# Two groups of tiled products per batch instead of three, with the scores and the slot reads moved into the h banks

## The chip, the cores and the metric

One core of one Trainium2 chip. The metric is device microseconds (us) of one execution; each kernel was run several times, and medians and ranges are given. Engines: PE is TensorE, DVE is VectorE, ACT is ScalarE, POOL is GpSimd, SP is SyncE (it issues most transposing transfers here). In the profile's lines PEld is the loading of weights into PE. The granted clock is the share of PE's full clock that the chip allowed. A run is called slow when it is more than 1.5% above the fastest of the same kernel. Medians and ranges are over all runs of a kernel unless it says otherwise; slow runs are left out of the ratios.

## The reference, cut to what matters

Eight batches of eight heads. Each batch has 512 tokens and 32 state slots per head. Tokens read the slots, slots read the tokens, and all rows then go through a two-layer expert with a squared ReLU.

```python
# x (8, 8, 512, 64), state (8, 8, 32, 64)
scores  = x @ state^T / sqrt(64);  a  = softmax(scores);   xread = a  @ state
scores2 = state @ x^T / sqrt(64);  a2 = softmax(scores2);  sread = a2 @ x
out = concat([xread, sread], axis=2)              # rows (8 * 544, 512)
h = out @ w_in                                    # (., 2048)
g = s * relu(h)**2 + b
return g @ w_out                                  # (., 512)
```

## The kernel before

Three things carry the argument.

First, `xread @ w_in` is never formed as such. With M = state @ w_in (per head, 32 rows each), h = a @ M. So each batch needs M in four pieces (`att_M`, PSUM tile `Mps`), the scores transposed (`att_T`, tile `T`), the slot reads (`att_V`, tile `V`), and then 16 blocks of h (`mm1_x`, two matmuls of 512 columns each). M, T and V are made with tiled products: several small matmuls side by side in the PE array. They are the only matmuls in a steady batch that use another tiling.

Second, the second layer uses a scheme of seven products of half-size sums (`fast_items`, tiles `oA`, `oB`, `oC`, sums `s`, weight sums `wd`). These 112 matmuls of 256 columns of the previous batch are spread over the current batch, seven after each h block.

Third, PSUM (the memory into which PE writes its results) is full. It has eight banks:

```python
psA = tile_pool(name="psA", bufs=2)   # "att": 2 buffers of two banks: T, Mps, V, D
psH = tile_pool(name="psH", bufs=2)   # "h":   2 buffers of one bank:  h blocks
psO = tile_pool(name="psO", bufs=2)   # "o":   2 buffers of one bank:  oA, oB, oC
```

What reads V is VectorE, which scales the slot reads by 1 / row sum (called "the scaling" below):

```python
def att_V(b):
    ps = att_ps([P, NG, D], FP32, f"V_{b}")          # a large buffer
    ...                                              # 32 matmuls of 64 columns
    for g in range(NG):
        nc.vector.tensor_scalar(a["sr"][:, g], ps[:, g], a["rq"][:, g : g + 1], None, ALU.mult)
```

VectorE also makes the token softmax of the next batch from the transposed exponentials ET (called "the shares"):

```python
def att_shares(b):
    with tc.issue_after(G["last"]):
        nc.vector.reduce_sum(den, ET_s, axis=X)               # 1.21 us
        nc.vector.reciprocal(inv, den)                        # 0.35 us
        nc.vector.tensor_mul(a["aT"], ET_s, inv.broadcast)    # 1.23 us
```

It is used from batch `NDT` = 4 on; earlier batches take their denominators from a matmul (`att_D`). The work of batch s (nb = s + 1 is the next batch) was placed so:

```python
at(3, att_T(nb));  at(3, att_M(nb, 0))        # group 1, after h(3)
at(7, att_M(nb, 1));  at(7, att_M(nb, 2))     # group 2, after h(7)
at(8, att_shares(nb));  at(9, att_a4_dma(nb))
at(10, att_V(s));  at(10, att_M(nb, 3))       # group 3, after h(10)
if s == 2: at(0, stT_dma)                     # transposed state of batches 3..7
...
for f in range(16):
    mm1_x(s, f)                               # h block f
    ... pieces of f ...
    ... seven second-layer matmuls of batch s - 1 ...
```

The softmax here doesn't subtract the row's maximum and nothing guards it: scores larger than these inputs give would overflow.

Of the kernel before, what the change touches and what calls it, by code (L numbers as in the profile page):

```python
# [14 lines left out]
def kernel(  # L15
# [10 lines left out]
    nc = tc.nc  # L26
# [19 lines left out]
    NDT = 4  # L46
# [162 lines left out]
    def att_T(b, gs):  # L209
        a = A[b]  # L210
        n = len(gs)
        T = att_ps([P, 2, 512], FP32, f"T_{b}_{gs[0]}")
        for q in range(NQ):
            for i, g in enumerate(gs):
                h = head_of(g, q)
                for m in range(2):
                    mm(
                        T[32 * q : 32 * q + 32, m, 256 * i : 256 * i + 256],
                        st_of(b, h, m),
                        a["xT"][64 * m : 64 * m + 64, h].rearrange("p k t -> p (k t)"),  # L220
                        tp=(64 * m, 32 * q),
                    )
        if gs[0] == 0:
            a["E"] = apool.tile([P, NG, S], FP16, name=f"E_{b}", tag="E", bufs=3)
            a["rs"] = apool.tile([P, NG], FP32, name=f"rs_{b}", tag="rs", bufs=4)
        for i, g in enumerate(gs):
            nc.scalar.activation(  # L227
                a["E"][:, g, :].rearrange("p (m t) -> p m t", m=2),
                T[:, :, 256 * i : 256 * i + 256],
                AF.Exp,  # L230
                scale=scale,
                accum_out=a["rs"][:, g : g + 1],
            )
# [44 lines left out]

    def att_M(b, c, how):
# [17 lines left out]
        if how == "split":  # L297
            nc.vector.tensor_copy(dst[:, 0], two[0])  # L298
            (nc.vector.tensor_copy if c in (0, 3) else nc.scalar.copy)(dst[:, 1], two[1])
        elif how == "act":  # L300
            nc.scalar.copy(dst, ps)  # L301
        else:
            nc.vector.tensor_copy(dst, ps)

    def att_ET(b):
        a = A[b]
        a["ET"] = apool.tile([P, NG * SCH, P], FP16, name=f"ET_{b}", tag="ET", bufs=3)
        nc.sync.dma_start_transpose(out=a["ET"], in_=a["E"].rearrange("p g t -> p (g t)"))
        a["rq"] = apool.tile([P, NG], FP32, name=f"rq_{b}", tag="rq", bufs=4)
        nc.vector.reciprocal(a["rq"], a["rs"])  # L310

    def att_V(b):
        a = A[b]
        ps = att_ps([P, NG, D], FP32, f"V_{b}")
# [43 lines left out]
    def mm1_close(key, hps, ntok, f):  # L358
# [3 lines left out]
        if key == 0 and f in (1, 5):  # L362
            nc.vector.tensor_scalar(r16[:, f % 2], hps, 0.0, None, ALU.max)
        else:
            nc.scalar.activation(r16[:, f % 2], hps, AF.Relu)  # L365
        if f % 4 == 0:
# [293 lines left out]
    with tc.manual_schedule(engines={ET.PE, ET.SP, ET.Pool}):  # L660
# [90 lines left out]
        def pieces(s):  # L751
# [5 lines left out]

            if s == 1:
# [3 lines left out]
                at(0, lambda: att_ET(1))  # L762
                at(8, lambda: att_xT_dma(3))
# [18 lines left out]
            if s == 2:  # L782
                at(0, stT_dma)
            if nb < B:
                at(3, lambda: att_T(nb, [0, 1]))
                at(3, lambda: att_M(nb, 0, "act"))
                at(4, lambda: att_ET(nb))
                if s in (2, 3):
                    at(4, lambda: att_xT_dma(nb + 1))
                if s >= 3 and s + 3 < B:  # L790
                    at(13, lambda: att_xT_dma(s + 3))
                if nb < NDT:
                    at(5, lambda: att_D(nb, [0, 1]))
                else:
                    at(8, lambda: att_shares(nb))
                    at(9, lambda: att_a4_dma(nb))
                at(7, lambda: att_M(nb, 1, "act"))
                at(7, lambda: att_M(nb, 2, "act"))
# [4 lines left out]
            at(10, lambda: att_V(s))  # L803
# [4 lines left out]
            if nb < B:  # L808
                at(10, lambda: att_M(nb, 3, "act"))
# [8 lines left out]
        for s in range(1, B):  # L818
# [13 lines left out]
            for f in range(NKF):  # L832
                mm1_x(s, f)
# [80 lines left out]
```

## Time and profile before

| | before |
|---|---|
| median of 3 runs | 210.69 us (210.08 to 210.84) |
| profiled span, granted clock | 208.0 us, 1.00 |
| PE / DVE / ACT / POOL busy | 96% / 78% / 60% / 18% |
| batch 2 (first h to first h) | 23.24 us |
| batches 3, 4, 5, 6 | 21.27 us each |
| from the first h of batch 7 to the last matmul | 43.50 us |

The lines themselves are in the prediction. A batch is measured from its first h matmul to that of the next. A "gap" in this document is the start of a matmul, less the start of the run of matmuls before it and its streaming time (0.216 us for 512 columns, 0.109 us for 256). The profile's own "idle" column is some 0.16 us smaller, because it models the end of a matmul later.

One more view of the kernel before is needed for the comparison. It is the timeline of VectorE in batch 4 around the scaling (columns: start, duration, engine, line, operation, output and input). The V matmuls of this batch began at 110.60 us.

```profile
110.02 1.23 DVE L265 TENSOR_TENSOR aT<-ET,inv 128x1024 f16<-128x1024 f16 x1
111.17 0.68 DVE L371 TENSOR_TENSOR g<-r 128x1024 f16<-128x1024 f16 x1
111.77 0.74 DVE L528 SCALAR_TENSOR_TENSOR osb<-oC,s_bc,u 128x512 f32<-128x512 f32 x1
112.43 0.47 DVE L328 TENSOR_SCALAR sr<-V,rq 128x64 f16<-128x64 f32 x2
```

Here 2.30 us pass from V's first matmul to the end of the scaling. V lies in one of the two large buffers and the next batch's T takes it only after the boundary.

### The profile page before, as it was taken

What the parts mean: (1) busy time and instruction counts of PE and PEld (TensorE: products, weight loads), DVE (VectorE), ACT (ScalarE), POOL (GpSimd) and SP (SyncE); (2) the same over time, 40 slices, a digit from 0 to 9 for tenths busy, and PEclk for the clock granted to TensorE, in tenths of its full rate; (3) what the DMA queues carried; (4) which work ended last, traced back from release to release, by engine and by line L of the source; (5) the groups of instructions that cost most, each with busy time, mean ns of one, the idle gap of its engine ahead of it and who ended that gap; (6) DMA issues with size and microseconds to landing.
All of it is one profiled execution on the core that took longest, in us unless ns stands there. A gap on an engine that the chain in (4) does not pass through costs nothing.

```text
span 208.0 us, 4757 instructions
## 1 busy us (share of the span) xinstructions
PE 199.5 (96%) x1947; PEld 129.4 (62%) x1947; DVE 162.1 (78%) x282; ACT 125.3 (60%) x218; POOL 37.6 (18%) x64
## 2 busy tenths in 40 slices
PE   7888999999899999999999999999999999999992
PEld 2433343445566676667666766676667777788882
DVE  1587825978769796899779977998799877895862
ACT  3678865698489557765776477656774544533100
POOL 5970001501110330123011201120111012100210
PEclk9999999999999999999999999999999999999999
DMA  5999996999947299979833915231324111110143
GB/s 183 225 202 206 207 191 104 179 181 174 266 52 153 72 194 123 124 163 185 127 103 67 196 52 102 54 107 54 101 29 132 50 54 50 54 50 0 54 145 111
DMA packets 45946, 25.35 MB, mean 122 GB/s; under 512 B 30884, under 2 KB 43940, under 8 KB 45924
## 3 DMA queue, kind: packets, MB, share of 16 engines
q0 software_dynamic: 15536, 16.19, 38.8%
q1 hardware_dynamic: 29588, 8.49, 23.8%
q10 hardware_dynamic: 800, 0.36, 0.7%
q8 instruction: 15, 0.25, 0.5%
q14 instruction: 7, 0.06, 0.1%
HBM read 17.33 MB, written 8.91 MB: 126 GB/s over the span
## 4 chain that ended last, share of the span: by engine, by line
PE 82%; DVE 6%; DMA 6%; ACT 4%; issue 1%; POOL 0%; SPq 0%; POOLq 0%
PE h L70 23%; PE oB L70 17%; PE oC L70 12%; PE oA L70 10%; PE o L70 6%; PE Mps L70 4%; DMA wi<-in_moe_w_in_dram 4%; PE h_sr L70 3%; DMA stT_all<-st 2%; ACT r L365 2%; DVE g L371 1%; PE T L70 1%; PE oB_sr L70 1%; PE V L70 1%; DVE M L298 1%; PE oA_sr L70 1%
## 5 line engine op out<-in xcount | busy, mean ns | idle before, releaser
L365 ACT ACTIVATE r<-h 128x512 f16<-128x512 f32 x126 | 74.4, 601 | 52.0 <-PE h L70 51.4
L70 PE MATMUL h<-a,M 128*128 128x512 f16 x256 | 75.0, 379 | 0.9 <-DVE M L298 0.6
L371 DVE TENSOR_TENSOR g<-r 128x1024 f16<-128x1024 f16 x64 | 44.1, 691 | 16.0 <-ACT r L365 15.8
L70 PEld LDWEIGHTS <-s 128*128 128x128 f16 x448 | 42.8, 98 | 19.3 <-issue 3.7
L70 PEld LDWEIGHTS <-g 128*128 128x128 f16 x400 | 38.0, 98 | 18.9 <-issue 2.9
L536 POOL DMA_DIRECT2D out_dram<-osb x27 | 18.2, 675 | 125.5 <-DVE osb L528 120.3
L70 PE MATMUL oB<-wd,s 128*128 128x256 f16 x224 | 32.7, 273 | 0.0
L70 PE MATMUL oA<-wo,g 128*128 128x256 f16 x224 | 31.6, 273 | 0.1
L70 PEld LDWEIGHTS <-M 128*128 128x128 f16 x256 | 24.6, 98 | 10.9 <-DVE M L298 1.6
L301 ACT CAST M<-Mps 128x1024 f16<-128x1024 f32 x27 | 26.8, 1017 | 1.4 <-PE Mps L70 0.8
L70 PE MATMUL oC<-wd,s 128*128 128x256 f16 x112 | 16.5, 273 | 0.0
L70 PE MATMUL o<-wo,g 128*128 128x512 f16 x64 | 16.3, 380 | 0.0
L70 PE MATMUL oB<-wd,g 128*128 128x256 f16 x112 | 15.9, 273 | 0.0
L70 PE MATMUL oC<-wo,s 128*128 128x256 f16 x112 | 15.3, 273 | 0.0
L365 ACT ACTIVATE r_sr<-h_sr 128x256 f16<-128x256 f32 x16 | 6.1, 382 | 8.4 <-PE h_sr L70 8.4
L227 ACT ACTIVATE E<-T 128x512 f16<-128x512 f32 x16 | 9.4, 596 | 1.2 <-PE T L70 1.1
L471 DVE TENSOR_TENSOR s<-s,g 128x1024 f16<-128x1024 f16 x14 | 9.7, 691 | 0.4
L70 PE MATMUL h_sr<-srdT,wi 128*128 128x256 f16 x64 | 9.6, 273 | 0.0
L465 DVE TENSOR_TENSOR s<-g 128x1024 f16<-128x1024 f16 x14 | 9.6, 685 | 0.0
L473 DVE TENSOR_TENSOR s<-g,s 128x1024 f16<-128x1024 f16 x14 | 9.6, 684 | 0.0
L469 DVE TENSOR_TENSOR s<-g,g 128x1024 f16<-128x1024 f16 x14 | 9.6, 683 | 0.0
L528 DVE SCALAR_TENSOR_TENSOR osb<-oC,s_bc,u 128x512 f32<-128x512 f32 x12 | 8.9, 746 | 0.5 <-PE oC L70 0.5
(102 smaller groups left out, 187.4 us busy)
## 6 DMA issues: line engine op xcount, KB each, us to landing
out_dram<-osb POOLq DMA_DIRECT2D x31, 256.0 KB, 2.8
xn<-in_x_dram POOLq DMA_DIRECT2D x7, 512.0 KB, 7.0
wi<-in_moe_w_in_dram POOLq DMA_DIRECT2D x4, 512.0 KB, 9.2
wo<-in_moe_w_out_dram POOLq DMA_DIRECT2D x4, 512.0 KB, 15.9
xf<-in_x_dram SPq DMA_DIRECT2D x2, 512.0 KB, 4.8
out_dram<-osb_sr SPq DMA_DIRECT2D x8, 32.0 KB, 1.6
out_dram<-osb_sr ACTq DMA_DIRECT2D x8, 32.0 KB, 1.7
out_dram<-osb_last SPq DMA_DIRECT2D x2, 128.0 KB, 1.9
```

The source lines that it names most:

```text
L70: return nc.tensor.matmul(out, lhsT, rhs, start=start, stop=stop, tile_position=tp, is_transpose=is_transpose, skip_group_check=True,)
L227: nc.scalar.activation(a["E"][:, g, :].rearrange("p (m t) -> p m t", m=2), T[:, :, 256 * i : 256 * i + 256], AF.Exp, scale=scale, accum_ou ...
L298: nc.vector.tensor_copy(dst[:, 0], two[0])
L301: nc.scalar.copy(dst, ps)
L365: nc.scalar.activation(r16[:, f % 2], hps, AF.Relu)
L371: nc.vector.tensor_mul(gt[:, f % 4 - 1 : f % 4 + 1], r16, r16)
L465: nc.vector.tensor_sub(o, a11, a21)
L469: nc.vector.tensor_add(o, a21, a22)
L471: nc.vector.tensor_sub(o, SQ[b, 1, j], a11)
L473: nc.vector.tensor_sub(o, a12, SQ[b, 2, j])
L528: nc.vector.scalar_tensor_tensor(osb, acc[bank], s_bc, add, ALU.mult, ALU.add)
L536: nc.gpsimd.dma_start(dst[j][:, :, n0 : n0 + NH], osb)
```

## The change

Its intent: switching the array between tilings costs time, so do it twice a batch and not three times. For that the scores take the two h banks (one per half, exponentials split in four), V takes one h bank, and the two large buffers are left for two pieces of M. Batch 3 uses the transposed softmax too (`NDT` = 3), and the state transposes are issued a batch earlier. The core of the diff:

```diff
-    NDT = 4
+    NDT = 3
@@ att_T
+        one_bank = b >= NDT
+        if one_bank:
+            Ts = [psH.tile([P, NG, S // 2], FP32, tag="h", name=f"T_{b}_{m}") for m in range(2)]
...
+        if one_bank:                       # four exponentials of 256 columns
+            for m in range(2):
+                for g in gs:
+                    nc.scalar.activation(a["E"][:, g, 256 * m : 256 * m + 256], Ts[m][:, g, :], AF.Exp, ...)
@@ att_V
-        ps = att_ps([P, NG, D], FP32, f"V_{b}")
+        if b >= NDT - 1:
+            ps = psH.tile([P, NG, D], FP32, tag="h", name=f"V_{b}")
+        else:
+            ps = att_ps([P, NG, D], FP32, f"V_{b}")
@@ pieces(1)
+                at(7, stT_dma)
                 at(8, lambda: att_xT_dma(3))
@@ pieces(s), s >= 2
-            if s == 2:
-                at(0, stT_dma)
-                at(3, lambda: att_T(nb, [0, 1]))
-                at(3, lambda: att_M(nb, 0, "act"))
+                ahead(4, lambda: att_M(nb, 0, "later"))
+                ahead(4, lambda: att_T(nb, [0, 1]))
+                ahead(4, lambda: att_M(nb, 1, "later"))
...
-                at(7, lambda: att_M(nb, 1, "act"))
-                at(7, lambda: att_M(nb, 2, "act"))
-            at(10, lambda: att_V(s))
+            ahead(10, lambda: att_V(s))
+                ahead(10, lambda: att_M(nb, 2, "later"))
+                ahead(10, lambda: att_M(nb, 3, "later"))
-                at(10, lambda: att_M(nb, 3, "act"))
@@ the loop over f
+                for fn in todo_s.get((f, "ahead"), []):
+                    fn()
+                if s > 1 and f >= 4:       # the seven second-layer matmuls now come before h(f)
+                    for fn in items[f]:
+                        fn()
+                    items[f] = []
                 mm1_x(s, f)
```

"later" means that the matmuls of M come in the group and the copy out of PSUM a few h blocks after it. The shares stay at f = 8 and 9.

More of the change, by code (lines that the diff above doesn't have):

```diff
@@ L210, in att_T @@
         a = A[b]
-        n = len(gs)
-        T = att_ps([P, 2, 512], FP32, f"T_{b}_{gs[0]}")
+        one_bank = b >= NDT
+        if one_bank:
+            Ts = [psH.tile([P, NG, S // 2], FP32, tag="h", name=f"T_{b}_{m}") for m in range(2)]
+        else:
+            T = att_ps([P, 2, 512], FP32, f"T_{b}_{gs[0]}")
+            Ts = [T[:, m, 0 : 256 * len(gs)].rearrange("p (g t) -> p g t", t=256) for m in range(2)]
         for q in range(NQ):
@@ L217, in att_T @@
                     mm(
-                        T[32 * q : 32 * q + 32, m, 256 * i : 256 * i + 256],
+                        Ts[m][32 * q : 32 * q + 32, i, :],
                         st_of(b, h, m),
@@ L224, in att_T @@
             a["E"] = apool.tile([P, NG, S], FP16, name=f"E_{b}", tag="E", bufs=3)
-            a["rs"] = apool.tile([P, NG], FP32, name=f"rs_{b}", tag="rs", bufs=4)
+            n = 2 * NG if one_bank else NG
+            a["rs"] = apool.tile([P, n], FP32, name=f"rs_{b}", tag="rs", bufs=4)
+        if one_bank:
+            for m in range(2):
+                for g in gs:
+                    nc.scalar.activation(
+                        a["E"][:, g, 256 * m : 256 * m + 256],
+                        Ts[m][:, g, :],
+                        AF.Exp,
+                        scale=scale,
+                        accum_out=a["rs"][:, NG * m + g : NG * m + g + 1],
+                    )
+            return
         for i, g in enumerate(gs):
@@ L277, in att_a4_dma, with copy_M @@
         )
+    def copy_M(dst, ps):
+        with tc.issue_after(G["relu"]):
+            nc.scalar.copy(dst, ps)
     def att_M(b, c, how):
@@ L296, in att_M @@
         dst = a["M"][:, :, FC * c : FC * c + FC]
-        if how == "split":
+        if how == "later":
+            a["M", c] = lambda: copy_M(dst, ps)
+        elif how == "split":
             nc.vector.tensor_copy(dst[:, 0], two[0])
@@ L309, in att_ET @@
         a["rq"] = apool.tile([P, NG], FP32, name=f"rq_{b}", tag="rq", bufs=4)
-        nc.vector.reciprocal(a["rq"], a["rs"])
+        rs = a["rs"]
+        if b >= NDT:
+            rs = apool.tile([P, NG], FP32, name=f"rt_{b}", tag="rt")
+            nc.vector.tensor_add(rs, a["rs"][:, 0:NG], a["rs"][:, NG : 2 * NG])
+        nc.vector.reciprocal(a["rq"], rs)
     def att_V(b):
         a = A[b]
-        ps = att_ps([P, NG, D], FP32, f"V_{b}")
+        if b >= NDT - 1:
+            ps = psH.tile([P, NG, D], FP32, tag="h", name=f"V_{b}")
+        else:
+            ps = att_ps([P, NG, D], FP32, f"V_{b}")
         for g in range(NG):
@@ L365, in mm1_close @@
             nc.scalar.activation(r16[:, f % 2], hps, AF.Relu)
+            G["relu"] = nc.cur_bb.bb.instructions[-1]
         if f % 4 == 0:
@@ L756, in at, with ahead @@
                 out.setdefault(f, []).append(fn)
+            def ahead(f, fn):
+                out.setdefault((f, "ahead"), []).append(fn)
             if s == 1:
@@ L781, in pieces @@
                 at(13 if s == 2 else 2, lambda: load_x(s + 3))
-            if s == 2:
-                at(0, stT_dma)
             if nb < B:
-                at(3, lambda: att_T(nb, [0, 1]))
-                at(3, lambda: att_M(nb, 0, "act"))
+                ahead(4, lambda: att_M(nb, 0, "later"))
+                ahead(4, lambda: att_T(nb, [0, 1]))
+                ahead(4, lambda: att_M(nb, 1, "later"))
                 at(4, lambda: att_ET(nb))
-                if s in (2, 3):
+                at(4, lambda: A[nb]["M", 0]())
+                at(6, lambda: A[nb]["M", 1]())
+                if s == 3:
                     at(4, lambda: att_xT_dma(nb + 1))
-                if s >= 3 and s + 3 < B:
-                    at(13, lambda: att_xT_dma(s + 3))
-                if nb < NDT:
-                    at(5, lambda: att_D(nb, [0, 1]))
-                else:
-                    at(8, lambda: att_shares(nb))
-                    at(9, lambda: att_a4_dma(nb))
-                at(7, lambda: att_M(nb, 1, "act"))
-                at(7, lambda: att_M(nb, 2, "act"))
+                at(8, lambda: att_shares(nb))
+                at(9, lambda: att_a4_dma(nb))
+                if s == 2:
+                    at(9, lambda: att_xT_dma(nb + 1))
+                elif s + 3 < B:
+                    at(13, lambda: att_xT_dma(s + 3))
             if s == 2:
@@ L802, in pieces @@
                 at(12, lambda: att_srT_dma(1))
-            at(10, lambda: att_V(s))
+            ahead(10, lambda: att_V(s))
+            if nb < B:
+                ahead(10, lambda: att_M(nb, 2, "later"))
+                ahead(10, lambda: att_M(nb, 3, "later"))
+                at(10, lambda: A[nb]["M", 2]())
+                at(12, lambda: A[nb]["M", 3]())
             if s == last_b:
@@ L807, in pieces @@
                 at(12, lambda: att_srT_dma(s))
-            if nb < B:
-                at(10, lambda: att_M(nb, 3, "act"))
             if s == last_b:
```

## The prediction

> **What bounds the kernel now.** I read the page first, then the busy time by stretch, then the matmuls in order of time over one batch, then VectorE (DVE) at a batch boundary.
>
> The page and, with it, the list of waits:
>
> ```profile
> PE 199.5 (96%) x1947; PEld 129.4 (62%) x1947; DVE 162.1 (78%) x282; ACT 125.3 (60%) x218; POOL 37.6 (18%) x64
> ...
> PE 82%; DVE 6%; DMA 6%; ACT 4%; issue 1%; POOL 0%; SPq 0%; POOLq 0%
> ...
> PE T L70 <- DMA stT_all<-st: 0.8, 1, 0.8
> ```
>
> TensorE (PE) carries 82% of the chain that ended last, and the only wait that the change names is a single one of 0.8 us for the transposed state. A busy PE is not yet a full PE, so I took batches. A batch starts at its first h matmul: 52.26, 75.50, 96.77, 118.04, 139.32 and 160.59 us for batches 2 to 7. The stretches between them:
>
> ```profile
> 52.26:75.50 23.24, 22.42 (x261) 14.89 (x259) 18.66 (x33) 16.06 (x26) 3.50 (x5) 1.00 0.64 136
> 75.50:96.77 21.27, 21.27 (x227) 14.58 (x224) 18.68 (x31) 14.17 (x25) 3.61 (x5) 1.00 1.03 154
> 96.77:118.04 21.27, 21.27 (x226) 14.59 (x224) 18.67 (x31) 14.16 (x25) 3.60 (x5) 1.00 0.65 127
> ```
>
> (Columns after the length: busy PE, weight loads, DVE, ACT, POOL.) Three things to see: 21.27 us repeats to the hundredth, PE is never idle in it, and DVE is 18.7 of 21.3 us busy, 88%, so it has little room. That PE streams at its rate and doesn't merely look busy comes from the sum: 32 h matmuls at 0.216 us (the pairs below are 0.43 apart) are 6.9 us, 112 matmuls of 256 columns at 0.109 us (seven are 0.76) are 12.2 us, and 2.1 us is left for the tiled products T (scores), Mps and V. All of the steady stages can give lies in those 2.1 us. They are, in batch 4:
>
> ```profile
> 104.63 0.59 PE L70 MATMUL h<-a,M 128*128 128x512 f16 x2
> 105.06 0.82 PE L70 MATMUL oB<-wd,s 128*128 128x256 f16 x6
> ...
> 105.82 0.59 PE L70 MATMUL h<-a,M 128*128 128x512 f16 x2
> 106.35 0.63 PE L70 MATMUL Mps<-wi,stT_all 64*32 64x512 f16 x16
> 106.91 0.94 PE L70 MATMUL oC<-wd,s 128*128 128x256 f16 x7
> ...
> 110.60 0.42 PE L70 MATMUL V<-xn,ET 128*32 128x64 f16 x32
> 110.95 0.41 PE L70 MATMUL Mps<-wi,stT_all 64*32 64x512 f16 x8
> 111.29 0.94 PE L70 MATMUL oB<-wd,g 128*128 128x256 f16 x7
> ```
>
> Two h matmuls take 0.43 us, so the array was through at 106.25 and the tiled group began at 106.35: 0.10 us to enter. The 16 Mps need 2 x 0.213 us of streaming (eight tiles side by side, 512 columns each, at the h rate) and last 0.56: 0.13 us to leave. One group thus costs about 0.23 us beyond its work, three times a batch (T with one Mps; two Mps; V with one Mps).
>
> **What the Trainium skill says.** "TensorEngine Tiling (Array Packing)", section Tiling Modes (Key Properties): "Changing tiling mode (not just tile) drains the TensorE". The trace agrees, at the 0.10 and 0.13 us above. The same page, section Restrictions and Gotchas (PSUM Pressure), says that different row tiles may not use one PSUM bank at once; that is why the scores still take two banks when they move to h. "TensorE: Matmul & The Clock Gate", section Back-to-back issue gap, gives N/2.4 + 2.5 ns, or 216 ns for 512 columns: the trace has 0.43 us for two. No run shows the drain apart from its group.
>
> **The change part by part.**
> 1. Three groups become two: M0, T, M1 before h(4), and V, M2, M3 before h(10). Saved: one enter and leave, 0.23 us a batch. Batches 2 to 6 prepare a next batch: 5 x 0.23 = 1.15 us, all on PE, all on the path.
> 2. Batch 3 no longer forms its softmax denominators by matmul: two D matmuls in batch 2 go, 0.43 us of PE. ACT loses one log and one exponential of 1.0 us each (off the path), DVE loses a product (0.68) and gains what the later batches have, a sum, a reciprocal and a product of 1.21 + 0.35 + 1.23 us. DVE in batch 2 goes from 18.7 to about 20.8 us of some 22: 95%.
> 3. The state transposes: in the queue of SyncE they now stand ahead of the x transposes that were issued at 46.21 us, which waited for their load, in a queue idle from 39.5 us. The transposes take 4.6 us to land; they can be there by about 48 and are needed at 57. The gap before T of batch 3 was 57.45 - 56.06 - 0.43 = 0.96, of which 0.10 is the entry: 0.86 us saved.
>
> Sum of the gains: 1.15 + 0.43 + 0.86 = 2.44 us, which makes 208.2. Moving M's copies and splitting the exponentials (four of 256 columns for two of 512, an estimated 0.3 us more on ACT) is off the path, ACT being 67% busy. The score banks: the group begins about 0.8 us (seven matmuls) after h(3), M0 goes first, and h(3)'s activation is done by then. After T come M1 and seven products, 1.1 us in all, before h(4) wants a bank; two exponentials at an estimated 0.36 us and 0.3 us of delay need 1.0. It just fits.
>
> **What it gives back.** From h(4) on, the seven products of the previous batch now come before each h pair and no longer after. So h(15) comes 0.76 us later, measured from those products. At the boundary stands this chain on DVE:
>
> ```profile
> 96.84 0.69 DVE L371 TENSOR_TENSOR g<-r 128x1024 f16<-128x1024 f16 x1
> 97.44 0.75 DVE L554 SCALAR_TENSOR_TENSOR qa<-oA,s_bc,bias_bc 128x512 f32<-128x512 f32 x1
> 98.11 0.68 DVE L469 TENSOR_TENSOR s<-g,g 128x1024 f16<-128x1024 f16 x1
> 98.82 0.69 DVE L471 TENSOR_TENSOR s<-s,g 128x1024 f16<-128x1024 f16 x1
> ...
> 99.57 0.67 PEld L70 LDWEIGHTS <-s 128*128 128x128 f16 x7 [0.31 <-DVE s L471]
> ```
>
> h(15) began at 95.57, its products were wanted at 99.59, and the weights came at 99.57: no slack at all. In the new order PE is there 4 x 0.43 + 2 x 0.76 = 3.25 us after h(15). If qa moves ahead of g (its matmuls now end before h(15)), the chain is 1.27 (h to g) + 0.71 + 0.71 + 0.75 = 3.44. So I expect a new wait of 0.2 us at each of five boundaries, 1.0 us, and up to 0.3 in the tail, where such a chain exists too.
>
> **Rivals.**
> (a) No new wait at all: 208.2. For it: the items were placed with care, and PE-bound stages repeat exactly. Against it: the boundary chain has no slack.
> (b) DVE becomes what releases PE. V's result now lies in an h bank until DVE has scaled it. In batch 4, V began at 110.60 and its second scaling ended at 112.90, behind the 2.86 us of the shares. In the new order V comes about 1.2 us earlier against h(9) and the shares don't, so its bank may come free some 1.4 us after h(11) wants it. How bad depends on which of the two banks h(11) gets. A clue is that oB at 103.11 began while oA's bank was still to be read (osb, 103.31), so banks go to whichever is free, not in turn; then h(11) takes h(10)'s bank at 0.1 us of delay, perhaps 0.2 more for h(12). Five times 0.1 to 0.3 is 0.5 to 1.5 us; five times 1.4, 7 us, would be the bad end, 217.
> (c) In batch 2 there is a third tiled group, V of batch 1, whose bank M3 needs 2.0 us later. If the scaling stands behind batch 3's new shares, PE waits about 1.7 us there, once; I give this a little over half.
> (d) The state transposes, going out earlier, delay the load of x for batch 3 and with it its transposes. Landing at most 8.5 us after 46.21, these have over 2 us to spare: unlikely.
>
> **Range and chances.** 2.44 us of gain is sure work removed; 1.0 at the boundaries I count in full; about 0.2 for the tail, and I weigh (b) and (c) at half or less of their middle values because the placing looks tuned: 0.5 + 0.5 together, less 0.5 since a late PE at one wait shortens the next. Net 2.44 - 1.0 - 0.2 - 0.5 = 0.74, rounded up a little for that tuning: 209.8 us, 0.9 off 210.69. The best case is 208.2; two bad waits give 212 to 213. Range 207.9 to 212.3. Faster by 2% would be below 206.5, beyond the sum of all gains: 2%. Slower by 2% is above 214.9, which takes the bad end of (b): 4%.
>
> **What would show it.** Right: batches 3 to 6 take 21.27 - 0.23 + the waits; two tiled groups a batch, each with 0.10 and 0.13 around it; T of batch 3 without its wait; a wait for the second-half sums (L471) of about 0.2 us at the third product run of each batch. If that wait isn't there and batches take 21.04, (a) holds. If h(11) or h(12) waits for DVE's scaling of V and batches take 22 or more, (b). If the last Mps of batch 2 waits for a scaling, (c). The prediction is wrong if the group overhead doesn't fall with the number of groups, or if DVE's order at the boundary puts qa behind g, which makes each wait 0.85 us.

## The result, and the profile after

The changed kernel took 217.25 us (median of 4 runs, 216.91 to 218.45, all fast). The kernel before took 210.76 us in the same rounds. The ratio is 1.0324 (95% interval 1.0278 to 1.037): slower. Ratios here are the mean time of one kernel's fast runs over that of the other's fast runs of the same rounds, so they are not quite the ratio of the medians quoted. The predicted range ended at 212.3.

The page of the changed kernel, its busy times and the chain that ended last:

```profile
PE 200.9 (93%) x1945; PEld 129.6 (60%) x1945; DVE 163.4 (76%) x289; ACT 123.9 (57%) x236; POOL 37.6 (17%) x64
...
PE 53%; DVE 28%; ACT 8%; issue 6%; DMA 3%; DVEq 0%
```

PE's share of the chain fell from 82% to 53%, and VectorE's rose from 6% to 28%. VectorE is no busier as a share of the span than before (76% against 78%). It has become what PE waits for, without being full.

The busy times by batch of the changed kernel, batches 2 to 5 (columns as in the prediction; batch 6 took 22.61 us):

```profile
52.48:75.60 23.12, 22.05 (x259) 14.87 (x257) 19.67 (x36) 13.71 (x27) 3.42 (x6) 1.00 0.62 120
75.60:98.47 22.87, 21.44 (x225) 14.57 (x224) 18.90 (x33) 14.29 (x28) 4.77 (x7) 1.00 0.94 164
98.47:122.31 23.84, 21.61 (x225) 14.57 (x224) 18.73 (x32) 14.29 (x28) 3.17 (x5) 1.00 0.66 112
122.31:144.92 22.61, 21.44 (x225) 14.58 (x224) 18.64 (x32) 14.29 (x28) 2.70 (x4) 1.00 0.39 90
```

Batches that took 21.27 us, with PE busy all the time, now take 22.6 to 23.8, with PE idle for more than a microsecond. VectorE's work in them is the same 18.6 to 18.9 us. The list of waits of the changed kernel names the cause (columns: total, times, longest):

```profile
PEld L70 <- DVE sr L357: 7.1, 5, 2.0
PE h L70 <- DVE sr L357: 4.7, 4, 1.7
PE oB L70 <- DVE s L501: 1.2, 5, 0.5
DVE den L278 <- DMA ET<-E: 1.1, 1, 1.1
PE Mps L70 <- DVE sr L357: 1.0, 1, 1.0
```

An h matmul waits four times for `sr`, the scaling that empties V's bank. The third product run (oB) waits five times for the half sums. M's last piece waits once for the scaling of batch 1. In the timeline of PE in batch 5 of the changed kernel one sees which h block it is:

```profile
135.16 0.59 PE L70 MATMUL h<-a,M 128*128 128x512 f16 x2
135.68 0.42 PE L70 MATMUL V<-xn,ET 128*32 128x64 f16 x32
136.03 0.63 PE L70 MATMUL Mps<-wi,stT_all 64*32 64x512 f16 x16
136.59 0.94 PE L70 MATMUL oB<-wd,g 128*128 128x256 f16 x7
137.36 0.59 PE L70 MATMUL h<-a,M 128*128 128x512 f16 x2
...
138.12 0.60 PE L70 MATMUL oC<-wo,s 128*128 128x256 f16 x4
139.70 0.60 PE L70 MATMUL h<-a,M 128*128 128x512 f16 x2 [0.98 <-DVE sr L357]
```

The group itself is as planned: V, then two pieces of M, in one stretch. h(10) at 137.36 gets the free h bank. h(11) could have begun at 138.12 + 4 x 0.109 = 138.56; it began at 139.70, a gap of 1.14 us. VectorE's timeline in the same stretch says why:

```profile
135.45 1.21 DVE L278 TENSOR_REDUCE den<-ET 128x32 f32<-128x1024 f16 x1
136.58 0.74 DVE L558 SCALAR_TENSOR_TENSOR osb<-oC,s_bc,u 128x512 f32<-128x512 f32 x1
137.24 0.34 DVE L280 RECIPROCAL inv<-den 128x32 f16<-128x32 f32 x1
137.50 0.63 DVE L401 TENSOR_TENSOR g<-r 128x1024 f16<-128x1024 f16 x1
138.04 1.21 DVE L281 TENSOR_TENSOR aT<-ET,inv 128x1024 f16<-128x1024 f16 x1
139.17 0.47 DVE L357 TENSOR_SCALAR sr<-V,rq 128x64 f16<-128x64 f32 x2
```

VectorE works without a pause and in a fixed order. V is complete at about 136.0, but the scaling stands behind the three steps of the shares, an eviction and a square, and ends at 139.64. The scaling takes 0.47 us; V's bank is held for 3.96 us from its first matmul. Before it was 2.30 us, and in a bank that nobody needed.

At the boundary to batch 6 the chain of squares and half sums looks so on VectorE in the changed kernel:

```profile
145.25 0.74 DVE L584 SCALAR_TENSOR_TENSOR qa<-oA,s_bc,bias_bc 128x512 f32<-128x512 f32 x1
145.91 0.68 DVE L401 TENSOR_TENSOR g<-r 128x1024 f16<-128x1024 f16 x1
146.62 0.69 DVE L499 TENSOR_TENSOR s<-g,g 128x1024 f16<-128x1024 f16 x1
147.35 0.69 DVE L501 TENSOR_TENSOR s<-s,g 128x1024 f16<-128x1024 f16 x1
```

and so on PE:

```profile
147.31 0.59 PE L70 MATMUL h<-a,M 128*128 128x512 f16 x2
148.10 0.94 PE L70 MATMUL oB<-wd,s 128*128 128x256 f16 x7 [0.19 <-DVE s L501]
```

As predicted, qa has moved ahead of g. The last half sum ends at 148.04. PE was through with h(2) at 147.31 + 0.43 = 147.74 and began its products at 148.10, a gap of 0.35 us.

The batches add up from these gaps. With -0.23 us for the group that went:

| batch | before | group and other gains | boundary | h(4) | wait of h(11), with oC before it | sum | measured |
|---|---|---|---|---|---|---|---|
| 3 | 21.27 | -0.23 | +0.61 | +0.08 | +1.14 | 22.87 | 22.88 |
| 4 | 21.27 | -0.23 | +0.35 | +0.08 | +1.89 + 0.48 | 23.84 | 23.84 |
| 5 | 21.27 | -0.23 | +0.35 | +0.08 | +1.14 | 22.61 | 22.61 |
| 6 | 21.27 | -0.23 | +0.35 | +0.08 | +1.14 | 22.61 | 22.61 |

In batch 4 the transposed exponentials landed late (the wait of `den` above), the shares and all behind them with it. In batch 2 the gains are larger (-0.84 for the state transposes' wait, -0.43 for the two D matmuls, -0.23 for a group) and +1.23 for M's last piece, 0.08 at h(11) and 0.06 at h(4) take nearly all of them back: 23.12 against 23.24. The tail is 0.55 us longer (44.05). The rest of the 7.6 us of span is 0.2 us ahead of batch 2 and 0.1 after the last matmul.

### The profile page after: what moved, and what is told of

It is laid out like the page before. It is cut to its first block, busy times and chain, and to the rows that moved or that the text cites. A ratio compares the mean times of both kernels' runs of the same rounds, so it can differ in the third digit from the quotient of the medians.

```text
span 215.6 us, 4780 instructions
## 1 busy us (share of the span) xinstructions
PE 200.9 (93%) x1945; PEld 129.6 (60%) x1945; DVE 163.4 (76%) x289; ACT 123.9 (57%) x236; POOL 37.6 (17%) x64
## 4 chain that ended last, share of the span: by engine, by line
PE 53%; DVE 28%; ACT 8%; issue 6%; DMA 3%; DVEq 0%
PE h L70 12%; PE oB L70 10%; PE o L70 7%; DVE g L401 7%; PE oA L70 6%; ACT r L394 5%; PE oC L70 3%; DVE s L499 3%; DMA ET<-E 3%; PE h_sr L70 3%; DVE s L501 3%; PE warm_ps L70 3%; PE Mps L70 3%; DVE osb L558 2%; DVE aT L281 2%
## 5 line engine op out<-in xcount | busy, mean ns | idle before, releaser
L401 DVE TENSOR_TENSOR g<-r 128x1024 f16<-128x1024 f16 x64 | 43.6, 683 | 21.8 <-ACT r L394 21.6
L297 ACT CAST M<-Mps 128x1024 f16<-128x1024 f32 x20 | 20.1, 1007 | 0.0
L234 ACT ACTIVATE E<-T 128x256 f16<-128x256 f32 x20 | 7.4, 383 | 4.0 <-PE T L70 4.0
```

Of the source, the lines that this page charges most:

```text
L234: nc.scalar.activation(a["E"][:, g, 256 * m : 256 * m + 256], Ts[m][:, g, :], AF.Exp, scale=scale, accum_out=a["rs"][:, NG * m + g : NG * ...
L297: nc.scalar.copy(dst, ps)
L401: nc.vector.tensor_mul(gt[:, f % 4 - 1 : f % 4 + 1], r16, r16)
```

## The experiments

My theory after the result: VectorE's queue releases V's h bank too late, and h(11) happens to be given that bank. The rivals: the early state transposes disturb the transfers; the new order of products at the batch boundary costs the time; the tiled groups cost more than thought.

Each label is followed by its edit, what was expected, and what came. All timed runs are set against the kernel before on the same chip (medians between 209.97 and 210.51).

### Is it V's bank, and is it VectorE's queue?

**e12_bank.** The changed kernel with the two h banks named. They are handed out in turn, except that h(11) is given the bank that h(10) had. The instruction order on every engine was compared and is the same as in the changed kernel. The edit is shortened: T, V and the other users of the h banks go through `h_bank` as well.

```diff
-        return pool.tile([P, ntok], FP32, tag=tag, name=f"h_{key}_{f}")
+        same = key != "sr" and key >= 2 and f == 11
+        return h_bank([P, ntok], name, same)     # tags h0 and h1, one buffer each, in turn
```

> The changed kernel with the two h banks named, and the eleventh h chunk given the bank of the tenth and not that of V; the instructions of every engine and their order are the same. Theory (the bank that h(11) got is the step that failed): its wait of 1.14 us (1.89 in batch 4) falls to about 0.1, h(12) waits 0 to 0.2 for V's bank, and 0.8 to 1.0 us a batch comes back in batches 3 to 6, less if the boundary waits grow: 213 to 214. Rival (VectorE is late whatever the bank): the boundary waits grow by as much, 216.5 or more.

Measured: 215.01 us (213.93 to 216.29), ratio 1.0212 (1.0162 to 1.0263). PE in batch 5 of this kernel:

```profile
138.50 0.60 PE L70 MATMUL oC<-wo,s 128*128 128x256 f16 x4
139.02 0.59 PE L70 MATMUL h<-a,M 128*128 128x512 f16 x2
139.45 0.93 PE L70 MATMUL oC<-wo,s 128*128 128x256 f16 x7
```

The same h(11), after the same four products, has a gap of 0.08 us in place of 1.14 (138.94 to 139.02). h(12) waited 0.28 and 0.69 us in batches 3 and 4 and not at all in 5 and 6. So the bank handed to h(11) made the wait. But the batches came to 21.84 to 22.71 us, not to 21.5: the boundary gap went from 0.35 to between 0.52 and 0.78 us, and T of batch 3 waited 1.8 us for the transposed x in the profiled run. When PE is not held at h(11), it runs ahead into the next place where VectorE has not finished.

**e2_sr_act.** The changed kernel, with the scaling on ScalarE from batch 1 on.

```diff
-            nc.vector.tensor_scalar(a["sr"][:, g], ps[:, g], a["rq"][:, g : g + 1], None, ALU.mult)
+            nc.scalar.activation(a["sr"][:, g], ps[:, g], AF.Copy, scale=a["rq"][:, g : g + 1])
```

> The changed kernel with the scaling of V on ScalarE for batches 1 to 7 and not on VectorE; banks and the place of the shares as in the change. Theory (VectorE's order): the same 6.9 us go, less a little for ScalarE, whose two extra operations of an estimated 0.25 us stand near a copy of M of 1.0 us: 210 to 211.5. Rival (the lent bank): 216.3 or more. Second rival (any engine that empties the bank is late, since V comes before h(10)): part of it, 213 to 215.

Measured: two fast runs of 213.51 and 213.79 us, ratio 1.0162 (1.0139 to 1.0186); two slow ones, of 218.15 us and of 340.59 us. The latter, at a mean granted clock of 0.564, was the profiled one, so its trace says nothing of waits. A miss: the gain is less than expected (210 to 211.5). The number is that of the second rival (213 to 215, any engine empties the bank late); the next trace speaks against its mechanism.

**e2_again.** The same kernel once more, to get a trace.

> The changed kernel with V's scaling on ScalarE, once more, for a profile at full clock. Its fast runs were at 213.6. Expected in the trace: no wait before h(11) and before the last Mps of batch 2; the boundary waits for the second-half sums grown from 0.35 to 0.7 to 1.0 us, which makes batches of 21.8 to 22.1.

Measured: 217.04 us in its single run, at clock 1.00. No wait of h(11), so ScalarE doesn't empty the bank late; but the wait for the half sums has grown, and T has a new one. From the list of waits:

```profile
PE oB L70 <- DVE s L506: 2.7, 5, 0.8
PEld L70 <- DMA xT<-xn: 1.9, 1, 1.9
```

The transposed x of batch 3 came late, and batches 2 to 4 paid for that; by batch 6 a batch took 21.67. So this kernel scatters by over 3 us at full clock. That the landing of that transfer decides it is likely from this trace, but not shown: no fast run of e2_sr_act was profiled.

**e14_act_st9.** Both together: the scaling on ScalarE, and the state transposes issued after the x transposes of batch 3.

```diff
-                at(7, stT_dma)
                 at(8, lambda: att_xT_dma(3))
+                at(9, stT_dma)
```

> The changed kernel with two things together: V's scaling from batch 1 on by ScalarE instead of VectorE, and the state transposes issued after the x transposes of batch 3. Theory (the h bank that waits for VectorE's scaling is the main loss; the early state transposes are what scattered the run with ScalarE's scaling, 213.6 against 217.0): no h(11) wait and no wait of T for x, a boundary wait of 0.6 to 1.0 us as in the repeated run with ScalarE's scaling, batches 21.5 to 22.2, 212.5 to 214 us, with all runs within 1 us of each other. Rival (what remains after the bank wait goes is the boundary wait and others that grow by the same amount): batches 22.4 or more, 216 to 218 us.

Measured: 213.81 us (213.70 to 215.23, six runs, all fast), ratio 1.0165 (1.0127 to 1.0203). No wait of h(11), none of T for the transposed x (M's first piece, just ahead of T in batch 2, lost 0.28 us to the state transposes). The batches from 2 on were 22.76, 21.91, 22.41, 22.21 and 21.67 us; the boundary gaps were 0.46 to 0.97 us, with 0.14 more ahead of them in two batches. So about half of the loss went (the ratio fell from 1.0324 to 1.0165), and 3.4 us (213.81 against 210.43) remained. The theory's time came (212.5 to 214), and so did the rival's effect: the boundary took part of the gain. The median is that of the two fast runs of e2_sr_act, so the later place of the transposes narrowed the spread (1.5 us in six runs; under 1 was expected) and gained nothing beyond.

**e1_shares_late.** The changed kernel with the shares placed behind the scaling.

```diff
-                at(8, lambda: att_shares(nb))
-                at(9, lambda: att_a4_dma(nb))
+                at(10, lambda: att_shares(nb))
+                at(11, lambda: att_a4_dma(nb))
```

> The changed kernel with one thing moved: the shares of a batch (and the transpose that follows them) are issued two h chunks later, so that in VectorE's order the scaling of V comes before them and no longer after; V stays in an h bank. Theory (the order on VectorE holds the h bank of V): in batches 3, 5 and 6 the 1.14 us before h(11), in batch 4 the 0.48 and 1.89 us, and in batch 2 the 1.05 us before the last Mps go, 6.9 us in all: 217.3 becomes about 210.5. New risk: the transposed shares land near the next batch's start; if late, up to 1 us a batch is given back. Rival (the bank itself, one of only two h banks lent to V, is what costs): no more than 1 us is gained, 216.3 or more.

Measured: 217.63 us (216.06 to 221.0), ratio 1.0327 (1.0278 to 1.0376). Its list of waits (the profiled run was a slow one, 221.0):

```profile
PE oB L70 <- DVE s L501: 4.5, 5, 1.3
```

A miss; 210.5 was expected. The waits of h(11) and of M's piece were gone, and the time did not move. The number is the rival's (216.3 or more), but not its mechanism, a wait for the lent bank. The boundary gap rose from 0.35 to 0.97 us, with 0.15 and 0.25 us more at two other places, so that batches 5 and 6 took 22.48 us against 22.61; no fast run was profiled (in this one T also waited for the transposed x in batch 2, a gap of 3.2 us, and PE then ran at half rate for 3.7 us), but the fast ones, 216.06 to 218.19 us, are on the whole no shorter than the changed kernel's. The 2.8 us of the shares have to be done somewhere before the boundary; there is no room behind the scaling either.

**e3_v_att.** The changed kernel with V back in a large buffer.

```diff
-        if b >= NDT - 1:
+        if b >= B:          # never
             ps = psH.tile([P, NG, D], FP32, tag="h", name=f"V_{b}")
```

> The changed kernel with V of every batch back in one of the two large buffers and not in an h bank, all orders the same. Theory (VectorE's order): the wait doesn't go, it moves from h(11) to the last Mps of the group, which now needs V's buffer about 2 us sooner than h(11) did; 2 to 3 us in each of batches 3 to 6 in place of 1.1 to 2.4: slower still, 220 to 224. Rival (the lent h bank): 211 to 212, as the h banks alternate freely again.

Measured: 238.78 us (236.91 to 241.13), ratio 1.1328 (1.1276 to 1.138). The direction was expected, the size was not (220 to 224). PE in batch 5 of this kernel (the profiled run was the slowest, 241.13 us, but all four lie within 2% of each other):

```profile
150.17 0.41 PE L70 MATMUL Mps<-wi,stT_all 64*32 64x512 f16 x8
153.83 0.63 PE L70 MATMUL Mps<-wi,stT_all 64*32 64x512 f16 x8 [3.25 <-DVE sr L357]
154.39 1.67 PE L70 MATMUL oB<-wd,g 128*128 128x256 f16 x7
155.86 1.06 PE L70 MATMUL h<-a,M 128*128 128x512 f16 x2
```

The group's second piece of M now waits 3.3 us for the scaling, since V, M2 and M3 want three of two buffers. Then comes what I had left out: after the wait the seven products take 1.47 us (154.39 to 155.86) where they take 0.76 elsewhere, and PE runs at half its rate up to about 159.3. The Trainium skill, "TensorE: Matmul & The Clock Gate", Part 1 (What's actually happening), says that the clock drops to half after an idle window of about 3.4 us. This trace agrees: the gap was 3.45 us (150.17 + 0.21 to 153.83), and the mean granted clock of the run was 0.947. So the h bank for V is needed for two groups, and it is bought with the scaling's latency.

### Is it the new order of products?

**e4_order_end.** The changed kernel with the old order (products after h) for h(14) and h(15).

```diff
-                if s > 1 and f >= 4:
+                if s > 1 and 4 <= f < 14:
```

> The changed kernel with the products put after h again for the last two h chunks of a batch only, so that the last h of a batch comes one run of products sooner. Theory (the boundary wait comes from this order): 0.61 us in batch 3, 0.35 us in batches 4 to 7 and 0.4 in the tail go, 2.4 us in all: 214.8. The waits before h(11) stay at 1.1 to 1.9 us. Rival (the boundary wait is VectorE's backlog, shifted by the late shares): less than 0.8 us, 216.5 or more.

Measured: 218.68 us (217.49 to 220.41), ratio 1.0408 (1.0343 to 1.0474). A miss; 214.8 was expected. The boundary gap fell from 0.35 to 0.23 us only, and the waits of h(11) stayed at 1.14 and 1.87. Batches 5 and 6 gained 0.12 us each and, in the profiled run, batch 2 lost 2.6 us to a late transposed x. The order at the end of the batch is not where the time is.

### Is it the early state transposes, or the softmax of batch 3?

**e11_st9.** The changed kernel with the state transposes after the x transposes (the edit shown at e14_act_st9), nothing else.

> The changed kernel with the state transposes issued after those of x for batch 3, nothing else. If their early place is a part of the loss: 0 to 2 us faster than 217.3 and a narrower spread, T of batch 3 without a wait for x in every trace; the waits before h(11) and at the boundaries as they were: 216 to 217.

Measured: 218.02 us (217.79 to 218.83), ratio 1.0386 (1.0351 to 1.042). No faster; 216 to 217 was expected. The waits of h(11), 1.14 to 1.89 us, and at the boundary were the same, and T had no wait for x. That clears the early place of the main loss.

**b1_stT.** The kernel before, with only the state transposes moved to their new, early place.

> The kernel before with one part of the change alone: the state transposes issued in batch 1, ahead of the transposes of x for batch 3. My prediction's term: 0.86 us gained, 209.6. Theory from the traces of the changed kernel (there they took 10.5 to 14.6 us to land and not 4.6, and the x transposes behind them were issued at 48.2 to 51.3 and not 46.2 us): the wait changes hands, from none to over 2 us in T of batch 3, so 209.6 in the best execution and up to 212.5 in others, with a wider spread than the kernel before.

Measured: three fast runs of 209.52 to 210.28 us, ratio 0.9996 (0.9961 to 1.0032), and two slow ones of 215.12 and 218.40 us. In the slow profiled run the state transposes took 16.2 us to land and T waited 5.1 us for the transposed x of batch 3. The gain is nothing and the risk is there.

Where the transposes stand in the queue of SyncE, kernel before:

```profile
46.21 5.08 SPq L204 DMA_TRANSPOSE xT<-xn  x1
51.39 1.26 SPq L308 DMA_TRANSPOSE ET<-E  x1
52.83 2.24 SPq L162 DMA_TRANSPOSE stT_all<-st  x1
```

and changed kernel:

```profile
39.80 1.75 SPq L162 DMA_TRANSPOSE stT_all<-st  x1
48.27 4.80 SPq L204 DMA_TRANSPOSE xT<-xn  x1
```

Issued at 39.80 the state transposes took 10.5 us to land (4.6 us before), and the transposes of x, which wait for x's own load, were issued 2.1 us later than before. The two loads of x that were under way took 10.6 us to land (median; 8.7 before). So it is in the other profiled runs at full clock: the x transposes were issued at 48.2 to 52.4 us with the early place and at 46.2 to 47.8 with the old or the later one, but for e14_act_st9 with 49.5. That the two slow each other is inferred from this; no run separates them.

**b5_stT_after_x.** The kernel before, with the state transposes moved forward, but to right behind the x transposes.

```diff
-            if s == 2:
-                at(0, stT_dma)
...
                 at(8, lambda: att_xT_dma(3))
+                at(9, stT_dma)
```

> The kernel before with the state transposes issued after those of x for batch 3 and before E of batch 2: they neither meet the load of x nor come last. Expected: issued at about 51.4, landed at 56 to 56.5, needed at 56.6, so the wait of 0.86 us shrinks to 0 to 0.3: 209.7 to 210.1 with no wider spread.

Measured: 209.65 us (209.06 to 209.80), ratio 0.9969 (0.9943 to 0.9996). T's wait in batch 2 was gone, and the batch took 22.37 us against 23.24.

**b5_again.** The same, with more rounds.

> The kernel before with the state transposes behind those of x for batch 3, with more rounds: 0.997 of the kernel before again, interval wholly under 1. If it is 1.000 within 0.002, the gain of 0.86 us in batch 2 is lost in the scatter of the start.

Measured: 209.39 us (208.94 to 209.87, six runs), ratio 0.9958 (0.9936 to 0.998). In the profiled run batch 2 had:

```profile
52.50:75.33 22.83, 22.43 (x261) 14.90 (x259) 18.59 (x33) 16.08 (x26) 3.51 (x5) 1.00 0.66 139
```

and a wait of 0.45 us was left in it. This beats both kernels, by 0.4% for the kernel before.

**b2_ndt3.** The kernel before with `NDT = 3` only.

> The kernel before with the number of batches that form denominators by matmul put from 4 to 3. In this kernel the number does nothing else: batch 3 gets its shares from VectorE, two D matmuls (0.43 us of PE) and two ScalarE passes go. If VectorE has room in batch 2: 0.43 us gained, 210.1. If it has none there, as the last runs say (an extra 0.68 us cost 0.35 a batch): PE waits 1 to 2 us in batch 2 and at its end, 211.5.

Measured: 213.65 us (fast runs 210.83 to 213.99, one slow of 214.38), ratio 1.012 (1.0045 to 1.0195). Batches 3 to 6 were untouched at 21.27. Batch 2 took 25.00 us: T waited 2.5 us for the state transposes, and another 0.56 came at an oC run behind the new shares. The 0.43 us of the D matmuls is real, but batch 2 has no room on VectorE or in the queue for what replaces them.

### How much room has VectorE?

**b3_dve_late.** The kernel before with one half difference of 0.68 us computed twice, at f = 9 in batches 3 to 7.

> The kernel before with one more VectorE operation a batch in batches 3 to 7, a difference of token halves done twice (128x1024, 0.68 us), placed after the shares. Theory A (no slack in this stretch): PE waits about 0.6 us more at each of five boundaries, 3.0 us: 213.2. Rival (VectorE at 88% has 2.6 us a batch to spare): under 0.5 us, 210.7 or less.

Measured: 212.02 us (211.73 to 212.38), ratio 1.0078 (1.0051 to 1.0104). A miss in size; 213.2 was expected. Each of batches 3 to 6 grew by 0.34 us, all of it at the oC run after h(11), which waited for an eviction:

```profile
PE oC L70 <- DVE osb L536: 0.7, 4, 0.2
```

**b4_dve_early.** The same with another half sum of 0.68 us, at f = 4, where I expected room.

> The same extra operation of 0.68 us a batch in the kernel before, but after the boundary's chain, where VectorE is idle for 0.9 us before h(3)'s product. Theory A: within 0.5 us of the kernel before, 210.2 to 210.7. If it costs about 3 us like the other, the share of VectorE as a whole is what counts and not the stretch.

Measured: 212.1 us (211.63 to 212.51), ratio 1.008 (1.005 to 1.0109). A miss; 210.2 to 210.7 was expected. Each of batches 3 to 6 grew from 21.27 to 21.79 us, batch 3 for one:

```profile
75.22:97.01 21.79, 21.43 (x226) 14.57 (x224) 19.17 (x32) 14.24 (x25) 3.61 (x5) 1.00 0.91 152
```

Of 0.68 us of extra work, 0.34 and 0.52 us came out as time: the slack at the two places was 0.34 and 0.16 us. So VectorE's 12% of idle time in a batch, spread over waits for PE and ACT, could not be used in one piece at either.

### Can two groups be had without the waits?

**e5_group8.** The changed kernel with the second group ahead of h(8), so that V comes before the shares.

```diff
-            ahead(10, lambda: att_V(s))
-                ahead(10, lambda: att_M(nb, 2, "later"))
-                ahead(10, lambda: att_M(nb, 3, "later"))
+            ahead(8, ...)              # all three; copies of M at 5, 8 and 10
-                at(8, lambda: att_V(1))
+                at(12, lambda: att_V(1))
```

> The changed kernel with its second tiled group (V, M2, M3) two chunks sooner, before h(8) and not h(10), M's copies sooner with it, and V of batch 1 later in batch 2. The shares stay; the scaling of V comes before them in VectorE's order. Theory A, formed after the first four runs (VectorE has no slack from h(7) to the next batch's h(2), so that a wait removed there comes back at the boundary): the waits before h(11) and the last Mps go, those for the second-half sums grow from 0.35 to about 1.0 us; batches of about 22.2 us in place of 22.6, 215 to 216. Theory B (the order of V's scaling alone): batches of 21.5, 211.

Measured: 214.41 us (fast runs 213.35 to 214.49, one slow of 217.4), ratio 1.0167 (1.0114 to 1.022). No wait of h(11), but boundary gaps of 0.71 us: batches of 21.82.

**e7_best.** That, with the products ahead of h at f = 4 only.

> As the one before, and products before h only at h(4), where the score banks need it; from h(5) on h comes first again, as in the kernel before. Theory A: h(15) and with it VectorE's last stretch come 0.76 us sooner and V's scaling is out of the way, so the boundary wait falls under 0.3 us: batches of 21.1 to 21.4 and 208.5 to 210.5, with the transposes of x for batch 3 as the open risk (up to 2.4 us in some runs). Rival (the later transposed scores hold the shares up, and PE waits whatever the order): batches of 22 us, 213 or more.

Measured: 215.06 us (214.92 to 217.39), ratio 1.0247 (1.0184 to 1.0311). A miss; 208.5 to 210.5 was expected. The boundary gap was zero, and in its place stood 0.30 us at h(5) and 0.66 us at the oC run after h(11): batches of 22.05.

**e10_best_st9.** That, with h(4) and h(5) both after their products, the shares one block later, the state transposes after x, and the half sums ordered ahead of the next square.

> Candidate that keeps the two groups: from the changed kernel, the second group before h(8); products before h only at h(4) and h(5); shares one chunk later, so that the third product's bank is emptied before them; the state transposes behind those of x for batch 3; and the half-sums ahead of the next batch's first product in VectorE's order. Theory A (all waits are VectorE's order and its lateness, each to be cleared by placing): batches 3 to 6 at 21.1 to 21.3, 208.5 to 210. If waits of 0.5 us or more a batch turn up in another place again, as in the last candidate (0.66 before the third product), VectorE's rate of work between h(7) and the next h(3) is the bound whatever the order: 212 or more.

Measured: 220.70 us (219.86 to 222.03), ratio 1.0506 (1.046 to 1.0552). A miss. The shares' transposed result came late for the next batch: the first h waited up to 3.8 us for it, 5.6 us in all. After the longest of these waits PE ran at half rate for some 5.5 us more (78.76 to 84.3).

**e13_best2.** e5_group8 with h(4) and h(5) after their products, the state transposes after x, the scaling on ScalarE, and one sum of VectorE's (qb) on GpSimd.

> Candidate: second group before h(8), products ahead of h only at h(4) and h(5), state transposes behind those of x, and two operations a batch taken off VectorE: V's scaling to ScalarE, and one sum of SBUF tiles (qa and the bias difference, 0.68 us) to GpSimd, 1.15 us a batch together. If VectorE's rate was what kept the two groups from paying: batches 3 to 6 at 21.1 to 21.3, batch 2 at 21.6 to 22, 208 to 209.5, ahead of the 209.65 of the kernel with its state transposes moved alone. If not: waits of 0.5 us a batch in a new place, 211 or more.

Measured: 212.47 us (211.50 to 212.82), ratio 1.0101 (1.0068 to 1.0134). A miss; 208 to 209.5 was expected. It is the best kernel with two groups that I found: batches of 21.4 to 21.7 us, boundary gaps of 0.20, and 0.10 to 0.64 us at the oC run (1.84 in batch 2). It doesn't reach the kernel before.

## Why the prediction was wrong, point by point

**The bound before.** Right in the sense that PE was full and VectorE 88% busy in a batch. But "it has little room" was then not carried into the sum. b3_dve_late and b4_dve_early put numbers to it: 0.34 and 0.16 us of slack at two places. (VectorE's load in batch 2 was put at 20.8 of some 22 us; it measured 19.67 of 23.12.)

**The gains.** Right, all three. The batches add up with 0.23 us per group, the D matmuls and T's wait went, 2.4 us in all. The group overhead falls with the number of groups; the rival "groups cost more than thought" is out.

**The boundary.** Right in kind and in the order of qa and g; the size was short. It cost 0.35 us at four boundaries and 0.61 at one, 2.0 us in place of 1.0. In batches 4 to 7 the missing 0.15 us is qa. The predicted chain started g 1.27 us after h(15), so at 144.49 + 1.27 = 145.76; VectorE was in qa until then and g began at 145.91.

**h(4).** "It just fits" was 0.08 us off, in each of batches 3 to 6. (The exponentials took 0.38 us each, not 0.36.)

**Rival (b): the failed step.** The working had the release of V's bank 1.4 us too late for h(11), and asked which bank h(11) gets. The prediction took a clue (banks go to whichever is free) and concluded that "h(11) takes h(10)'s bank at 0.1 us of delay". It takes V's. The trace shows 1.14 us in batches 3, 5 and 6 and 1.89 in batch 4, so what was called the bad end of (b), and was given 4%, is the result. e12_bank shows that this is the step: the other bank, the same order, and the gap is 0.08. The clue itself was misread. The oB products that begin at 103.11 take no new bank: they go on in the one that oB opened at 97.20 (in `fast_items` only products 1, 6 and 5 start a new one), so they say nothing of how banks are handed out. Nor is the layout the same in every batch. In batch 2 of the changed kernel h(11) did get what was predicted: it began, with a gap of 0.08 us, before V of batch 2 was scaled.

```profile
70.38 0.59 PE L70 MATMUL h<-a,M 128*128 128x512 f16 x2
...
70.87 0.47 DVE L357 TENSOR_SCALAR sr<-V,rq 128x64 f16<-128x64 f32 x2
```

Why V's bank is picked in batches 3 to 6 is not shown by any run. That the bad end's 217 lies so near the measured 217.25 is partly luck: it stood for five waits of 1.4 us, and there were four (5.3 us in all), while the boundary cost 2.0 us and not 1.0, (c) 1.2 us, and the oC run of batch 4 0.5 us that nobody had foreseen. What to take from it: the estimate of 1.4 us was good, and it was thrown away on a guess about an allocation. The range should have held both outcomes.

**Rival (c).** It came, at about 1.2 us of the 1.7.

**Rival (d).** Called unlikely. It didn't show in the profiled run of the change, but T waited for the transposed x in the profiled runs of e1_shares_late, e3_v_att, e4_order_end, e5_group8, e12_bank and e2_again, with gaps of 1.3 to 3.2 us, all with the early place, and by 5.1 us in the slow run of b1_stT; in e7_best, with the early place too, and with the later place (e10_best_st9, e11_st9, e13_best2, e14_act_st9) it didn't.

**The correction "less 0.5 since a late PE at one wait shortens the next".** Right, and larger than thought, and the reverse holds too: taking the 1.14 us away (e12_bank, e14_act_st9, e5_group8) let the boundary gap grow from 0.35 to between 0.5 and 1.0. So the loss is not one wait but a lack of slack: PE, made 0.23 us faster per batch, was put closer behind VectorE at three places, the bank of V being the worst.

In total: the ratio of 1.0324 fell to 1.0212 with the bank alone (e12_bank) and to 1.0165 with the scaling on ScalarE and the state transposes behind those of x (e14_act_st9), a third and a half of the loss. The bank by name together with the later transposes was not run. What remains of it lies at the boundary and at single late transfers. The Trainium skill, "TensorEngine Tiling (Array Packing)", section PSUM Bottleneck, would have pointed there: it says that tiling speeds up TensorE but not the emptying of PSUM, and to use both ScalarE and VectorE for that. The runs agree: the scaling on ScalarE took the wait away and was worth about half of the loss (1.0324 to 1.0162 in the fast runs of e2_sr_act).

What stays open: why the layout gives h(11) V's bank in batches 3 to 6 and h(10)'s in batch 2; why the boundary gap is 0.56 in some batches of e14_act_st9 and e2_again and 0.97 in others; and what brought a whole run of e2_sr_act to half clock.

## What to carry to other kernels

When a change saves time on a full engine by packing its work, list for every buffer in it who empties it, what stands ahead of that reader in its engine's queue, and which later instruction gets the buffer; take the worst allocation unless it is fixed by name. Test the slack of a nearly full second engine by giving it one instruction twice, at the place where the change would lean on it: here 0.68 us of extra work cost 0.34 to 0.52 us at the two places tried, more than the 0.23 us that the change saved in a batch. Move a transfer forward only to where it doesn't pass in front of another that is already waited for.

## What the Trainium skill lacked or had wrong

- "TensorEngine Tiling (Array Packing)", Tiling Modes (Key Properties), says that a change of mode drains the array but has no size for it. Here a group cost 0.10 us to enter and 0.13 us to leave, and one group fewer gave 0.23 us a batch.
- The same page, PSUM Bottleneck, speaks of the emptying as a matter of throughput. Here its place in the queue decided: 0.47 us of work held a bank for 3.96 us, with VectorE 82% busy in the batch (18.64 of 22.61 us).
- "TensorE: Matmul & The Clock Gate", Part 1: its idle window of about 3.4 us agrees with e3_v_att (a gap of 3.45 us, then half rate for about 5.5 us), and in b2_ndt3 a gap of 2.6 us was followed by full rate. But in e1_shares_late a gap of 3.2 us was enough: half rate came about 1 us after it. No run explains the execution at half clock throughout (340.59 us, mean granted clock 0.564), whose first batch already took 21.9 us in place of 15.6.
- In none of the pages that I looked up: the landing time of one and the same transposing transfer, which was 4.6 us in the kernel before and 10.5 to 16.2 us when it was issued next to a load of x.
